# Second MoE layer in groups of four PSUM banks, with weight addresses kept in registers

## The chip, the cores and the metric

The kernel runs on one core of a Trainium2 chip. The metric is the device time of one execution in microseconds (us). Before the change it is 2098.32 us, the median of three runs (2098.08 to 2103.15). TensorE is called PE below (its weight loads PEld), VectorE DVE, ScalarE ACT, GpSimd POOL, SyncE SP.

## The reference

Three layers in a row over 14336 tokens of 192 numbers: a causal convolution with 7 softmax-normalised taps per head, a mixture of experts (MoE) in which each token goes to its best expert of eight, and a second MoE in which each token goes to its two best by noisy logits.

```python
x = _attn_ref(x, weight)                  # 7 taps, 8 heads of 24
# layer 1: expert_idx = argmax(x @ w_gate)
    h = np.maximum(xe @ w1[e], 0.0)       # 192 -> 1024
    out[mask] = gate_w * (h @ w2[e])      # 1024 -> 192
# layer 2: two best of logits + log1p(exp(x @ w_noise)) * noise
    h = np.maximum(x[mask] @ w1[e], 0.0)
    out[mask] += top2_w[mask, k, None] * (h @ w2[e])
```

All is float32, and the kernel gets near it with pairs of float16 numbers (a high and a low part).

## The kernel before

Tokens are scattered into DRAM tables with one region per expert (`rows1` for layer 1, `rows2` for layer 2), by POOL's indirect DMAs. A planner in the Python code (`spawn`, `pump`, `clk`) writes the order of every engine's instructions; a wait in that order is the hardware's. The MoE work runs as a list of steps (`seq`), each of T tokens of one expert: T is 512, 256 or 128. A step of layer 1 gets its rows as soon as an epoch of tokens is counted; layer 2 begins with four steps of 512 whose second weights have buffers of their own (`own`, the bridge), then 38 steps of 512 (19 regions of 1024), 7 of 512, 7 of 256 and 21 of 128. Layer 1 has 2 steps of 512, 45 of 256 and 21 of 128.

`load` (line 906) is SP's part of a step: the weights `w1t` (1 MB, three buffers), the tokens transposed into `xT` (three blocks of 128 rows: the high parts of inputs 0 to 127; high and low parts of inputs 128 to 191; low parts of 0 to 127), and, where `nb` is 2, `x3`, which holds the high parts of inputs 128 to 191 in its upper 64 rows.

`mm1` (line 939) makes the hidden layer. It has eight chunks of 128 hidden units. A chunk takes four matmuls over all 128 rows and one over the 64 rows that are left (low part of the weights by the high part of inputs 128 to 191). With `nb` 2 (all steps of layer 2 over 128 tokens, and the 512-token steps of layer 1) two chunks go to two PSUM banks `ph`, and their 64-row products stand next to each other, one on the lower 64 rows of the array and one on the upper, from `x3`. With `nb` 1 the fifth product is done over 128 rows. `parts` evicts a bank: ACT writes the relu as float16 into `h`, DVE the rest that float16 lost. There are four `ph` banks.

`mm2` (line 992) multiplies the step before by the second weights: per 128 tokens eight chunks of three matmuls, into a bank `py` (two of them). The weights of all experts lie in one tile `w2r`. Which expert it is is only known at run time: `st.re` is a register that PE loads from the table `g.tb` (`value_load`, line 947), and each matmul takes an address worked out from it. `run` (line 1160) alternates: a group of `mm1` for step n, a share of `mm2` for step n-1, then the evictions, then `finish`, where ACT scales `py` into `y` and POOL scatters it (layer 2: an adding scatter into the output; the first scatter of a step waits until those of the step before have landed).

Of the kernel before, what the change touches and what calls it, by code (L numbers as in the profile page):

```python
# [9 lines left out]
F16 = mybir.dt.float16  # L10
# [3 lines left out]
OP = mybir.AluOpType  # L14
# [4 lines left out]
P = 128  # L19
N, D, E, F = 14336, 192, 8, 1024  # L20
# [23 lines left out]
SLACK = {"dve": 0.4, "act": 0.4, "pool": 1.5, "pe": 1.2, "hw": 1.5, "dma": 6.0}  # L44
HOP = 0.15
BRIDGE = 4


def n_full(avail, t):
# [8 lines left out]
def conv_moe_moe2_kernel(ctx: ExitStack, tc: tile.TileContext, xh, cw, cwb, wg, w11, w21, w2t, w12, w22, out):  # L58
# [574 lines left out]
    def table(g, total):  # L633

        m, t, steps = g.m, g.t, g.k
        u = used[m][ucur[m]]
        L = lambda nm, shape=(P, E), dt=F32: sm.tile(list(shape), dt, name="tb" + nm, bufs=1)
        av = L("av")
        v.tensor_sub(av, total, u)
        yield vv()  # L640
        if g.last:
            v.tensor_scalar(av, av, float(t - 1), None, op0=OP.add)
            yield vv()
        ai = L("ai", dt=I32)
        v.tensor_copy(ai, av)
        yield vv()
        gi = L("gi", dt=I32)
        v.tensor_single_scalar(gi, ai, -t, op=OP.bitwise_and)
        yield vv()
        gf = L("gf")  # L650
        v.tensor_copy(gf, gi)
        yield vv()
        cm = L("cm", (P, E, E))
        v.tensor_tensor(cm, gf[:, None, :].to_broadcast([P, E, E]), upto, op=OP.mult)
        yield vv()
        ci = L("ci")
        v.tensor_reduce(ci, cm, op=OP.add, axis=AX.X)
        yield vv()
        cx = L("cx")
        v.tensor_sub(cx, ci, gf)  # L660
        pos = L("pos", (P, 1))
        v.tensor_scalar(pos, part, float(t), None, op0=OP.mult)
        yield vv()
        oh = L("oh")
        v.tensor_scalar(oh, ci, pos, None, op0=OP.is_gt)
        rb = L("rb")
        v.tensor_add(rb, u, reg_e)
        yield vv()
        v.scalar_tensor_tensor(oh, cx, pos, oh, op0=OP.is_le, op1=OP.mult)
        v.tensor_sub(rb, rb, cx)  # L670
        yield vv()
        val = L("val", (P, 4))
        v.scalar_tensor_tensor(cm[:, 0, :], rb, pos, oh, op0=OP.add, op1=OP.mult, accum_out=val[:, 0:1])
        v.scalar_tensor_tensor(cm[:, 1, :], iota_e, 1.0, oh, op0=OP.mult, op1=OP.mult, accum_out=val[:, 1:2])
        v.scalar_tensor_tensor(cm[:, 2, :], sE[m], 1.0, oh, op0=OP.mult, op1=OP.mult, accum_out=val[:, 2:3])
        yield vv()
        if g.last:
            v.tensor_reduce(val[:, 3:4], oh, op=OP.add, axis=AX.X)
            v.tensor_scalar(val[:, 3:4], val[:, 3:4], -float(DUMMY), float(DUMMY), op0=OP.mult, op1=OP.add)
            v.tensor_add(val[:, 0:1], val[:, 0:1], val[:, 3:4])  # L680
        tb = cst.tile([P, 3], I32, name=g.tag + "tb")
        v.tensor_copy(tb[:, 0:2], val[:, 0:2])
        v.tensor_scalar(tb[:, 2:3], val[:, 1:2], float(FC * 2 * DG), None, op0=OP.mult)
        dg = L("dg", (P, 2, steps))
        for j in range(2):
            v.tensor_scalar(dg[:, j, :], ident[:, :steps], val[:, 1 + j:2 + j], None, op0=OP.mult)
        yield vv()
        tk = L("tk")
        v.tensor_scalar(tk, cx, -1.0, float(steps * t), op0=OP.mult, op1=OP.add)
        v.scalar_tensor_tensor(tk, tk, 0.0, gf, op0=OP.max, op1=OP.min)  # L690
        nu = used[m][1 - ucur[m]]
        v.tensor_add(nu, u, tk)
        ucur[m] ^= 1
        g.tb, g.ready = tb, clk["dve"]
        yield on("pe", "dve")
        pb = yield from bank("pr")
        t_.matmul(pb[:, :2 * steps], ones32, dg.rearrange("p a b -> p (a b)"), start=True, stop=True)
        yield on("dve", "pe")
        g.bc = cst.tile([P, 2, steps], F32, name=g.tag + "bc")
        v.tensor_copy(g.bc.rearrange("p a b -> p (a b)"), pb[:, :2 * steps])  # L700
        held["pr"] = False
# [202 lines left out]
    def load(st):  # L904
        T, S = st.T, st.T // P
        g = st.g
        rows = rows1 if g.m == 0 else rows2
        rv = q_.value_load(g.tb[st.i:st.i + 1, 0:1], min_val=0, max_val=DUMMY if g.last else DUMMY - g.t)
        if st.first:
            re = q_.value_load(g.tb[st.i:st.i + 1, 1:2], min_val=0, max_val=E - 1)  # L910
            st.w[0] = wk.tile([P, 4 * F], F16, name="w1t", bufs=3)
            q_.dma_start(st.w[0], w1s[g.m].rearrange("e p f -> (e p) f")[bass.ds(re * P, P), :])
            if g.own:
                st.w[1] = prep[0].tile([P, FC * 2 * D], F16, name="w2t", bufs=BRIDGE)
                q_.dma_start(st.w[1], w2s.rearrange("e p f -> (e p) f")[bass.ds(re * P, P), :])
        row = bass.ds(rv + st.skip, T) if st.skip else bass.ds(rv, T)
        if st.off == 0:
            st.b.xT = wk.tile([P, 3, 512], F16, name="xT", bufs=3)
            st.b.ax = wk.tile([P, 4, AUX], F32, name="ax", bufs=9)
        st.xT = st.b.xT[:, :, st.off * P:st.off * P + T]  # L920
        ins = [q_.dma_start_transpose(st.xT, rows[row, 0:HALF].bitcast(F16))]
        if st.nb == 2:
            if st.off == 0:
                st.b.x3 = wk.tile([P, 512], F16, name="x3", bufs=3)
            st.x3 = st.b.x3[:, st.off * P:st.off * P + T]
            ins.append(q_.dma_start_transpose(st.x3[:, None, :], rows[row, 32:96].bitcast(F16)))
        st.ax = st.b.ax[:, st.off:st.off + S, :]
        ins.append(q_.dma_start(st.ax, rows[row, HALF:ROW].rearrange("(s p) w -> p s w", p=P)))
        for i in ins:
            row_read(g.m, i, g.deps)  # L930
        st.at = clk["done"]

    def chunk(st, k):

        n = 512 // st.T
        f, j = divmod(k, n)
        return f // st.nb * n + j + f % st.nb * FC // 2

    def mm1(st, f):


        T, n = st.T, 512 // st.T
        if f == 0:
            st.h = wk.tile([P, 2, 512 * FC // n], F16, name="h", tag="h", bufs=2)
            st.hv = st.h.rearrange("p k (c t) -> p k c t", c=FC)
        if f == st.nb % 2 and not st.g.own:
            st.re = t_.value_load(st.g.tb[st.i:st.i + 1, 2:3], min_val=0, max_val=(E - 1) * FC * 2 * DG)
        st.ph = [ps_h.tile([P, 512], F32, name="ph") for _ in range(st.nb)]
        x = lambda k: st.xT[:, k, :]
        for j in range(n):  # L950
            o = [ph[:, j * T:(j + 1) * T] for ph in st.ph]
            ws = []
            for b in range(st.nb):
                c = chunk(st, (f + b) * n + j)
                w = [st.w[0][:, k * F + c * P:k * F + (c + 1) * P] for k in range(4)]
                t_.matmul(o[b], w[0], x(0), start=True, stop=False)
                t_.matmul(o[b], w[0], x(2), start=False, stop=False)
                t_.matmul(o[b], w[1], x(0), start=False, stop=False)
                t_.matmul(o[b], w[2], x(1), start=False, stop=False)
                ws.append(w[3])  # L960
            if st.nb == 1:
                t_.matmul(o[0], ws[0], x(1), start=False, stop=True)
            else:
                t_.matmul(o[0], ws[0][:64], x(1)[:64], start=False, stop=True)
                t_.matmul(o[1], ws[1][64:], st.x3[64:], start=False, stop=True)

    def parts(st, f):
        hs = slice(f * 512, (f + 1) * 512)
# [7 lines left out]
    emptied = deque([0.0] * 4, maxlen=4)  # L976
    finished = []

    w2flat = w2r.rearrange("p e c -> p (e c)")

    def mm2(st, lo, hi):

        for qn in range(lo, hi):
# [3 lines left out]
            dd = D if st.g.m else DG  # L987
            py = st.py[:, :dd]
            hs = slice(s * P, (s + 1) * P)
            cw = chunk(st, c)  # L990
            if st.g.own:
                w = [st.w[1][:, (2 * cw + k) * D:(2 * cw + k + 1) * D] for k in range(2)]
            else:
                off = st.re + cw * 2 * dd
                w = [w2flat[:, bass.ds(off + k * dd if k else off, dd)] for k in range(2)]
            t_.matmul(py, st.hv[:, 0, c, hs], w[0], start=(c == 0), stop=False)
            t_.matmul(py, st.hv[:, 0, c, hs], w[1], start=False, stop=False)
            t_.matmul(py, st.hv[:, 1, c, hs], w[0], start=False, stop=(c == FC - 1))
# [156 lines left out]
    def run(seq):  # L1155
# [12 lines left out]
        for n, st in enumerate(seq + [None]):  # L1168
# [9 lines left out]
            for f in range(0, ns, nb):  # L1178
                ahead(n + 3)
                if st is not None:  # L1180
                    clk["pe"] = max(clk["pe"], emptied[nb - 1])
                    mm1(st, f)
                    if st.g.m and f == ns - nb:
                        ahead(n + 4)
# [23 lines left out]
    def group(m, t, k, last, own, tag):  # L1208
        g = Step()
        g.m, g.t, g.k, g.last, g.own, g.tag, g.tb, g.bc, g.deps = m, t, k, last, own, tag, None, None, None  # L1210
        for i in range(k):
            w = [None, None]
            for skip in range(0, t, 512):
                st = Step()
                st.g, st.T, st.i, st.skip, st.w, st.first, st.end = g, min(t, 512), i, skip, w, skip == 0, None
                st.nb = 2 if t > P and (m or t == 512) else 1
                S = st.T // P
                if not bats or bats[-1].S + S > 4:
                    bats.append(Batch())
# [139 lines left out]
```

## Time and profile before

| | |
|---|---|
| median of the runs | 2098.32 us |
| the profiled execution | 2103.14 us, span 2101.1 us |
| PE busy | 1796.6 us (86%), 16031 matmuls |
| DVE, ACT, POOL busy | 946.8, 848.5, 834.3 us |
| granted TensorE clock, mean | 0.91 |

The rows below are read so. A row of the timeline gives the start, the length, the engine, the operation with the tile it writes, an arrow and what it reads, and how many like it follow each other; in square brackets stands the idle time before it and what ended it. "issue" means that nothing the profile shows was waited for. A matmul's length contains the time in which it fills and drains the array, so a row of n matmuls is (n-1) steps and one length long. `ph<-xT,w1t` is mm1, `py<-w2r,h` is mm2, `ph<-x,w1t` is a product with `x3`.

### The profile page before, as it was taken

The page shows a single profiled execution, that of the slowest core. Times are in us where ns is not written, and L with a number is a line of the kernel's source. Part 1 is how long each engine was busy: PE and PEld are TensorE (multiplying, and loading weights), DVE is VectorE, ACT ScalarE, POOL GpSimd, SP SyncE. Part 2 cuts the span into 40 slices and gives each one's busy share as a digit, 9 for nine tenths or more (in the row PEclk, how much of TensorE's full clock was granted, in tenths as well). Part 3 has the DMA queues.
Part 4 walks back from the last instruction along what each step waited for, and adds up shares of the span by engine and source line. Part 5 has one row for each costly group of instructions (what it writes and reads, how often), then busy time and mean ns, then how long its engine had stood idle before and what let it go on. Part 6 is the DMA issues. An engine that isn't in the chain of part 4 may idle for free. (4 is left out here: it accounts for less than half of the span.)

```text
span 2101.1 us, 51695 instructions
## 1 busy us (share of the span) xinstructions
PE 1796.6 (86%) x16031; PEld 1365.3 (65%) x16031; DVE 946.8 (45%) x3508; ACT 848.5 (40%) x1756; POOL 834.3 (40%) x1512
## 2 busy tenths in 40 slices
PE   4778867667868897877789999999999999999993
PEld 3547756556757674766656666666666666667893
DVE  6856644535456574443345433333333333333341
ACT  4745644444334453433333333333333333333331
POOL 1453454545443334353335433333333333343323
PEclk9768988878879898888899999999999999999996
DMA  7868655334458785545698545554554556667792
GB/s 251 281 204 233 205 169 140 109 106 140 144 190 257 225 257 152 163 161 187 192 258 233 102 78 96 85 101 86 88 96 77 102 83 117 116 107 148 203 273 51
DMA packets 320693, 329.04 MB, mean 157 GB/s; under 512 B 230718, under 2 KB 279108, under 8 KB 303296
## 3 DMA queue, kind: packets, MB, share of 16 engines
q1 hardware_dynamic: 258400, 236.98, 40.2%
q0 software_dynamic: 55184, 74.92, 18.3%
q10 hardware_dynamic: 6864, 13.83, 2.0%
q8 instruction: 159, 2.61, 0.5%
q14 instruction: 86, 0.70, 0.1%
HBM read 189.50 MB, written 96.08 MB: 136 GB/s over the span
## 5 line engine op out<-in xcount | busy, mean ns | idle before, releaser
L95 PE MATMUL ph<-xT,w1t 128*128 128x256 f16 (+4 forms) x5568 | 877.0, 303 | 91.4 <-issue 78.7
L95 DVE SCALAR_TENSOR_TENSOR h<-ph,h 128x512 f16<-128x512 f32 x700 | 462.9, 687 | 961.1 <-ACT h L95 899.1
L95 PE MATMUL py<-w2r,h 128*128 x8016 | 813.5, 255 | 75.7 <-issue 74.4
L95 PEld LDWEIGHTS <-h 128*128 128x128 f16 x8400 | 726.2, 100 | 164.7 <-issue 146.8
L95 PEld LDWEIGHTS <-w1t 128*128 128x128 f16 (+1 forms) x5800 | 485.2, 101 | 398.0 <-issue 216.1
L95 ACT ACTIVATE h<-ph 128x512 f16<-128x512 f32 x700 | 392.3, 594 | 682.2 <-PE ph L95 493.7
L95 POOL DMA_INDIRECT out_dram<-y,ax x231 | 361.0, 1563 | 607.4 <-ACT y L95 421.3
L95 POOL DMA_INDIRECT rows<-row,gdi x238 | 237.3, 997 | 214.7 <-issue 189.0
L95 ACT ACTIVATE y<-py,cf 128x192 f32<-128x192 f32 (+1 forms) x350 | 148.6, 424 | 385.0 <-PE py L95 259.7
L95 POOL DMA_INDIRECT rows<-row,di x128 | 125.9, 984 | 152.2 <-DVE di L95 36.9
L95 POOL MEMSET spacer<- 1x1 f32 x613 | 172.4, 281 | 0.1
L95 PE MATMUL ph<-x,w1t 64*128 64x512 f16 (+1 forms) x232 | 87.3, 376 | 0.1
L95 PE MATMUL ph<-x,band 118*112 118x96 f32 x512 | 70.3, 299 | 5.2 <-issue 3.8
L95 PEld LDWEIGHTS ph<-x,band 118*112 118x112 f32 x512 | 66.4, 213 | 7.9 <-issue 5.5
L95 ACT ACTIVATE x<-x,ras 112x192 f32<-112x192 f32 x128 | 49.0, 446 | 19.3 <-DVE rai L95 13.2
L95 POOL CAST row<-gix 128x8 f32<-128x8 uint32 (+1 forms) x30 | 6.9, 229 | 110.0 <-DVE gex L95 47.0
L95 ACT ACTIVATE y<-y,rbs 128x192 f32<-128x192 f32 x119 | 46.5, 445 | 6.9 <-DVE rbs L95 6.9
L95 ACT ACTIVATE rT<-ph 128x672 f16<-128x672 f16 x64 | 43.2, 729 | 15.0 <-PE ph L95 10.7
L95 PE MATMUL ph<-ident,row 112*128 112x112 f16 x384 | 33.3, 245 | 15.4 <-DVE row L95 6.4
L95 PEld LDWEIGHTS <-row 112*128 112x128 f16 x384 | 27.6, 116 | 21.5 <-issue 12.7
L95 DVE TENSOR_TENSOR row<-x,row 112x256 f16<-112x256 f32 x64 | 33.4, 554 | 13.1 <-ACT row L95 12.9
L95 ACT ACTIVATE x<-ph 112x384 f32<-112x384 f32 x64 | 28.2, 480 | 27.0 <-PE ph L95 13.5
(275 smaller groups left out, 1142.6 us busy)
## 6 DMA issues: line engine op xcount, KB each, us to landing
w1t<-w1s SPq DMA_DIRECT2D x126, 1024.0 KB
x<-in_xh_dram ACTq DMA_DIRECT2D x32, 400.0 KB
w1raw<-in_w_dram SPq DMA_DIRECT2D x8, 1536.0 KB
w2raw<-in_w_dram SPq DMA_DIRECT2D x16, 768.0 KB
out_dram<-pads SPq DMA_DIRECT2D x11, 960.0 KB
w1s<-w1raw POOLq DMA_DIRECT2D x16, 512.0 KB
w1s<-whalf SPq DMA_DIRECT2D x16, 512.0 KB
w2tr<-in_w2t_dram POOLq DMA_DIRECT2D x16, 384.0 KB
```

The source lines that it names most:

```text
L95: r = f(*a, **kw)
```

## The change

Steps of layer 2 over 128 tokens take four chunks to four banks at a time (`nb` 4). The four 64-row products of both pairs of chunks stand in the middle of the group: chunks 0 and 1, then lower, upper, lower, upper rows, then chunks 2 and 3. The two 512-token steps of layer 1 get `nb` 1: no 64-row products and no `x3`. The order of chunks is now plain, so `chunk` is gone. The table's third column holds a byte offset. After the first two matmuls of a step, PE loads it and works out 16 addresses into 16 registers (`addresses`); an mm2 matmul then takes its address from a register as it stands. The planner's `emptied[nb // 3]` looks at the second of the last four evictions for `nb` 4.

```diff
+W2_AT = 20480
...
-        v.tensor_scalar(tb[:, 2:3], val[:, 1:2], float(FC * 2 * DG), None, op0=OP.mult)
+        v.tensor_scalar(tb[:, 2:3], val[:, 1:2], float(4 * FC * DG), None, op0=OP.mult)
...
-        if st.nb == 2:
+        if st.nb == 4:
...
-    def chunk(st, k):
-
-        n = 512 // st.T
-        f, j = divmod(k, n)
-        return f // st.nb * n + j + f % st.nb * FC // 2
-
     def mm1(st, f):
...
-        if f == st.nb % 2 and not st.g.own:
-            st.re = t_.value_load(st.g.tb[st.i:st.i + 1, 2:3], min_val=0, max_val=(E - 1) * FC * 2 * DG)
         st.ph = [ps_h.tile([P, 512], F32, name="ph") for _ in range(st.nb)]
         x = lambda k: st.xT[:, k, :]
+
+        def w(b, j, k):
+            c = (f + b) * n + j
+            return st.w[0][:, k * F + c * P:k * F + (c + 1) * P]
+
+        out_ = lambda b, j: st.ph[b][:, j * T:(j + 1) * T]
+        def whole(b):
+            for j in range(n):
+                o = out_(b, j)
+                first = j == 0 and b < 2
+                t_.matmul(o, w(b, j, 0), x(0), start=first, stop=False, skip_group_check=True)
+                t_.matmul(o, w(b, j, 0), x(2), start=False, stop=False, skip_group_check=True)
+                if f == b == j == 0 and not st.g.own:
+                    addresses(st)
+                t_.matmul(o, w(b, j, 1), x(0), start=False, stop=False, skip_group_check=True)
+                t_.matmul(o, w(b, j, 2), x(1), start=False, stop=b > 1, skip_group_check=True)
+
+        if st.nb == 4:
+            whole(0)
+            whole(1)
+            for b in (0, 2):
+                for j in range(n):
+                    for i, (rows, src) in enumerate(((slice(0, 64), x(1)), (slice(64, P), st.x3))):
+                        t_.matmul(out_(b + i, j), w(b + i, j, 3)[rows], src[rows], start=b == 2 and j == 0,
+                                  stop=b == 0, skip_group_check=True)
+            whole(2)
+            whole(3)
+            return
         for j in range(n):
-            o = [ph[:, j * T:(j + 1) * T] for ph in st.ph]
-            ws = []
-            for b in range(st.nb):
-                c = chunk(st, (f + b) * n + j)
-                w = [st.w[0][:, k * F + c * P:k * F + (c + 1) * P] for k in range(4)]
-                t_.matmul(o[b], w[0], x(0), start=True, stop=False)
-                t_.matmul(o[b], w[0], x(2), start=False, stop=False)
-                t_.matmul(o[b], w[1], x(0), start=False, stop=False)
-                t_.matmul(o[b], w[2], x(1), start=False, stop=False)
-                ws.append(w[3])
-            if st.nb == 1:
-                t_.matmul(o[0], ws[0], x(1), start=False, stop=True)
-            else:
-                t_.matmul(o[0], ws[0][:64], x(1)[:64], start=False, stop=True)
-                t_.matmul(o[1], ws[1][64:], st.x3[64:], start=False, stop=True)
+            o = out_(0, j)
+            t_.matmul(o, w(0, j, 0), x(0), start=True, stop=False)
+            t_.matmul(o, w(0, j, 0), x(2), start=False, stop=False)
+            if f == j == 0 and not st.g.own:
+                addresses(st)
+            t_.matmul(o, w(0, j, 1), x(0), start=False, stop=False)
+            t_.matmul(o, w(0, j, 2), x(1), start=False, stop=False)
+            t_.matmul(o, w(0, j, 3), x(1), start=False, stop=True)
 
...
-    w2flat = w2r.rearrange("p e c -> p (e c)")
+    w2bytes = w2r.rearrange("p e c -> p (e c)").bitcast(mybir.dt.uint8)
+
+    def addresses(st):
+
+        pe = nc.tensor
+        first = pe.value_load(st.g.tb[st.i:st.i + 1, 2:3], min_val=0, max_val=4 * (E - 1) * FC * DG)
+        step = 2 * (D if st.g.m else DG)
+        st.wr = []
+        for k in range(2 * FC):
+            r = pe.alloc_register(f"w2at{len(addressed)}_{k}")
+            pe.reg_alu(r, first, W2_AT + k * step, op=OP.add)
+            st.wr.append(pe.snap(r, min_val=W2_AT, max_val=W2_AT + 4 * (E - 1) * FC * DG + k * step,
+                                 guaranteed_mod_val=0, out_of_modulus=32))
+        addressed.append(st)
+
+    addressed = []
 
     def mm2(st, lo, hi):
 
...
-            cw = chunk(st, c)
+            cw = c
             if st.g.own:
                 w = [st.w[1][:, (2 * cw + k) * D:(2 * cw + k + 1) * D] for k in range(2)]
             else:
-                off = st.re + cw * 2 * dd
-                w = [w2flat[:, bass.ds(off + k * dd if k else off, dd)] for k in range(2)]
+                w = [w2bytes[:, bass.ds(st.wr[2 * cw + k] - W2_AT, 2 * dd)].bitcast(F16) for k in range(2)]
             t_.matmul(py, st.hv[:, 0, c, hs], w[0], start=(c == 0), stop=False)
             t_.matmul(py, st.hv[:, 0, c, hs], w[1], start=False, stop=False)
             t_.matmul(py, st.hv[:, 1, c, hs], w[0], start=False, stop=(c == FC - 1))
...
-                    clk["pe"] = max(clk["pe"], emptied[nb - 1])
+                    clk["pe"] = max(clk["pe"], emptied[nb // 3])
...
-                st.nb = 2 if t > P and (m or t == 512) else 1
+                st.nb = 4 if m and t > P else 1
```

The instructions on PE at the start of a 512-token step of layer 2, where mm2 of the step before ends and mm1 begins; `ISA` is a register instruction. Before:

```order
L95 LDWEIGHTS h
L95 ISA
L95 MATMUL py<-w2r,h 128x192
L947 TENSOR_LOAD tb1024tb
L947 ISA x2
L95 LDWEIGHTS w1t
L95 MATMUL ph<-xT,w1t 128x512
L95 LDWEIGHTS w1t
L95 MATMUL ph<-xT,w1t 128x512
L95 LDWEIGHTS w1t
```

The same place now:

```order
L96 LDWEIGHTS w1t
L96 MATMUL ph<-xT,w1t 128x512
L96 LDWEIGHTS w1t
L96 MATMUL ph<-xT,w1t 128x512
L998 TENSOR_LOAD tb1024tb
L998 ISA x2
L96 LDWEIGHTS w1t
L1003 ISA
L1004 ISA
L1003 ISA
L1004 ISA
L1003 ISA
```

The register instruction ahead of each mm2 matmul is gone, and the load of the expert's offset, with seven register instructions instead of two, has moved behind two matmuls of mm1.

The 64-row products of a 512-token step on PE, from the last 128-row product ahead of them; the rows with `x` read `x3`. Before, where mm2 follows:

```order
L95 LDWEIGHTS w1t
L95 MATMUL ph<-xT,w1t 128x512
L95 LDWEIGHTS w1t
L95 MATMUL ph<-xT,w1t 128x512
L95 LDWEIGHTS w1t
L95 MATMUL ph<-x_20971,w1t 128x512
L95 LDWEIGHTS h
L95 ISA
L95 MATMUL py<-w2r,h 128x192
L95 LDWEIGHTS h
```

Now, where four such products stand together and mm1 goes on:

```order
L96 MATMUL ph<-xT,w1t 128x512
L96 LDWEIGHTS w1t
L96 MATMUL ph<-xT,w1t 128x512
L96 LDWEIGHTS w1t
L96 MATMUL ph<-x_24917,w1t 128x512
L96 LDWEIGHTS w1t
L96 MATMUL ph<-xT,w1t 128x512
L96 LDWEIGHTS w1t
L96 MATMUL ph<-x_24917,w1t 128x512
L96 LDWEIGHTS w1t
L96 MATMUL ph<-xT,w1t 128x512
L96 LDWEIGHTS w1t
```

A switch from 128-row to 64-row products and back stood after every two chunks, and stands after every second pair of them now.

## Rows read from the trace of the kernel before

**Rows 1.** The page of the profile: its head and the engines' busy time.

```profile
span 2101.1 us, 51695 instructions
...
PE 1796.6 (86%) x16031; PEld 1365.3 (65%) x16031; DVE 946.8 (45%) x3508; ACT 848.5 (40%) x1756; POOL 834.3 (40%) x1512
```

**Rows 2.** Busy time by stretches: start:end, length, five engines, PE clock, DMA share, GB/s.

```profile
1400.00:1500.00 100.00, 100.00 (x820) 66.55 (x820) 34.09 (x66) 36.34 (x73) 38.69 (x50) 1.00 0.52 89
```

**Rows 3.** The timeline of large steps of layer 2, a group of mm1 and mm2.

```profile
1404.03 2.15 PE L95 MATMUL py<-w2r,h 128*128 x24
1404.13 1.08 ACT L95 ACTIVATE h<-ph 128x512 f16<-128x512 f32 x2 [1.62 <-PE ph L95]
1404.76 1.29 DVE L95 SCALAR_TENSOR_TENSOR h<-ph,h 128x512 f16<-128x512 f32 x2 [2.85 <-ACT h L95]
1405.94 1.48 PEld L95 LDWEIGHTS <-w1t 128*128 128x128 f16 x8
...
1406.02 1.89 PE L95 MATMUL ph<-xT,w1t 128*128 128x512 f16 x8
...
1407.84 0.10 PEld L95 LDWEIGHTS <-w1t 64*128 64x128 f16 x2 [0.42 <-issue]
...
1411.98 0.39 PE L95 MATMUL ph<-xT,w1t 64*128 64x512 f16 x1
1411.98 0.39 PE L95 MATMUL ph<-x,w1t 64*128 64x512 f16 x1
1412.30 2.15 PE L95 MATMUL py<-w2r,h 128*128 x24
1414.36 2.21 PE L95 MATMUL ph<-xT,w1t 128*128 128x512 f16 x9
```

**Rows 4.** Groups of PE instructions by shape, whole span: count, busy us, mean ns, idle before.

```profile
L95 PE MATMUL ph<-xT,w1t 128*128 128x512 f16 x1632 | 391.0, 382 | 5.1 <-issue 4.7
L95 PE MATMUL ph<-xT,w1t 128*128 128x128 f16 x1680 | 121.5, 227 | 32.9 <-issue 30.4 <-PE py L95 0.5 <-PE pr L95 0.3
...
L95 PE MATMUL ph<-xT,w1t 64*128 64x256 f16 x28 | 7.8, 280 | 0.0
```

**Rows 5.** The timeline of PE in the 256-token steps of layer 2.

```profile
1906.49 4.90 PE L95 MATMUL py<-w2r,h 128*128 x48
1911.94 0.81 PE L95 MATMUL ph<-xT,w1t 128*128 128x256 f16 x6 [0.56 <-DMA w1t<-w1s]
```

**Rows 6.** The timeline of PE and POOL in the 128-token steps that end layer 2.

```profile
2024.11 1.15 PE L95 MATMUL py<-w2r,h 128*128 x12
2025.37 1.29 PE L95 MATMUL ph<-xT,w1t 128*128 128x128 f16 x20
...
1979.29 1.56 POOL L95 DMA_INDIRECT out_dram<-y,ax  x1 [2.80 <-ACT y L95]
...
2061.85 1.56 POOL L95 DMA_INDIRECT out_dram<-y,ax  x1 [2.63 <-ACT h L95]
...
2092.53 1.56 POOL L95 DMA_INDIRECT out_dram<-y,ax  x1 [3.32 <-issue]
```

**Rows 7.** Waits of PE from 250 to 1150 us: total us, times, longest.

```profile
PE ph L95 <- issue: 83.4, 115, 1.9
PE py L95 <- issue: 73.2, 95, 1.8
```

**Rows 8.** The timeline of PE and POOL over one of those stretches.

```profile
1008.20 1.23 PE L95 MATMUL py<-w2r,h 128*128 x12
1009.60 0.28 PE L95 MATMUL ph<-xT,w1t 128*128 128x128 f16 x2 [0.16 <-issue]
...
1013.39 0.22 PE L95 MATMUL ph<-xT,w1t 128*128 128x128 f16 x1 [1.21 <-issue]
...
1017.70 1.03 PE L95 MATMUL ph<-xT,w1t 128*128 128x128 f16 x8 [0.44 <-issue]
...
1006.05 0.99 POOL L95 DMA_INDIRECT rows<-row,gdi  x1 [6.13 <-issue]
...
1015.24 0.99 POOL L95 DMA_INDIRECT rows<-row,gdi  x1 [0.23 <-issue]
```

## The prediction

> **What bounds the kernel now.** I read the stretches first, then the timeline of the stretch with the most time, then the waits of PE, then the end. In layer 2 the stretch of 100 us has PE busy for all of it at clock 1.00, the others for 34 to 39 us [rows 2]. So from about 1150 to 1970 us time is what PE's instructions take one after another. In layer 1 PE is also what the order waits for, but with holes: from 250 to 1150 us it idles 83.4 + 73.2 = 156.6 us for nothing that the profile shows [rows 7]. One such hole runs from 1009.60 to 1017.70: a matmul or two in each 0.7 us or so [rows 8]. Over it POOL issues eight scatters back to back, 1006.05 to 1016.23 [rows 8]. The very end is neither: POOL's adding scatters of the 128-token steps wait for one another, 13 intervals from 1979.29 to 2061.85 at 6.35 us and 7 more to 2092.53 at 4.38 us [rows 6]. I work against the profiled execution, 2103.14 us (span 2101.1 [rows 1] and 2.0 outside); it is 4.8 us over the median of 2098.32, and a saving is taken off that median.
>
> **64-row products, large steps.** A full 512-column matmul takes (1.89 - 0.38)/7 = 0.216 us; 0.38 is one matmul's mean length [rows 3, 4]. The eighth should make way at 1406.02 + 8 x 0.216 = 1407.75, but the weights of the 64-row products are only loaded at 1407.84 [rows 3]: 0.095 us. The two products start together at 1411.98, and mm2 follows at 1412.30: 0.32 us for 0.216 us of columns, 0.104 us more [rows 3]. So a pair costs 0.216 us and its two edges 0.20. Now two pairs share the edges: 0.20 us less in each group of four, 0.40 in a step. There are 1632/32 = 51 steps of 512 [rows 4], 49 of them in layer 2: **19.6 us**. The two of layer 1 pay 40 full matmuls (8.64 us) where they paid 32 and four pairs with edges (8.58): nothing.
>
> What the trace of before does not show is one 64-row pair right behind another. If the second costs as much as the first with its edges, the gain is 0; if its weights are loaded behind the running pair, it is the 19.6. At full height the loads do run ahead: eight of them lie between 1405.94 and 1407.42, beside the matmuls of the same rows [rows 3]. That row is the nearest, so I take 19.6. [...]
>
> **Smaller steps of layer 2.** A 256-token step has four pairs (28 products of a kind in 7 steps [rows 4]), each with its edges before, and one run of four now: 3 x 0.20 x 7 = **4.2 us**.
>
> **Register instructions.** Each mm2 matmul had one ahead of it. In large steps that is hidden: 24 matmuls pass in 1.99 us, 0.083 each, their 192 columns' worth at the rate above [rows 3]. In a run of 48 it is not: (4.90 - 0.25)/47 = 0.099 [rows 5]. The new group has runs of 48 everywhere; without the instruction I put them at 0.083, with no gain or loss.
>
> Loading the offset stood between mm2 and mm1. There mm1 starts 2.06 us after mm2 did, against 1.99 [rows 3]: 0.07 us in each of 45 large steps, **3 us**. In 128-token steps the hole is larger: 2024.11 + 12 x 0.083 = 2025.11, and mm1 starts at 2025.37 [rows 6], 0.27 us. If layer 1's 21 such steps pay alike, as 1008.20 to 1009.60 for twelve matmuls says [rows 8], that is **5.7 us** on PE there. The 7 steps of 256 give about 1.9 at that price, less what a wait for `w1t` as at 1911.94 takes back [rows 5]: I keep **1**. The 21 steps at the end gain 5.7 on PE too, but POOL's chain behind them sets the end: **1**.
>
> The load now stands behind two matmuls, with five more register instructions. I cost it at nothing, because behind an mm2 without register instructions PE's queue should hold enough work. If that cover fails, it costs the 0.27 us hole plus five instructions at no more than 0.099 us, 0.77 us in each of 141 steps: 109 us. Ends 0 and 109; the large step, with 0.07 us left uncovered under the old load [rows 3], is the nearest row, and there the queue was fed more slowly than it will be.
>
> **Evictions.** Four banks instead of two now wait for ACT and DVE. Two take ACT 1.08 us and DVE 1.29 [rows 3], four about 3.2 with the first relu. The first two banks are complete in the middle of the group; the last one is done about 1.5 us after the group's end, and PE then has 48 mm2 matmuls, 4.0 us, before it needs banks 0 and 1. No wait; without that cover it would be up to 1.5 us in each of 98 groups. The `y` copies come behind the evictions on ACT, and their scatters behind them; POOL is busy 39 of 100 us [rows 2].
>
> **Holes of layer 1.** In a hole the instructions come at a fixed poor rate, so their number counts. mm2 falls from three per matmul to two: a third of its 73.2 us would be 24 us [rows 7], while mm1's 83.4 stays. A hole's end follows POOL's last scatter (1016.23, then 1017.70 [rows 8]), which the change does not touch, so I take half, **12 us**. Bounds: 0, and all 156.6.
>
> Sum: 19.6 + 4.2 + 3 + 5.7 + 1 + 1 + 12 = 46.5 us. 2098.3 - 46.5 = **2052 us** (the profiled execution would be 2057).
>
> **Rivals.**
> 1. The second pair pays its own edges: 19.6 + 4.2 = 24 us less gain, **2076**. For it: both edges stand at every pair in the trace. Against it: the edge comes with the change from 128 rows to 64, and between pairs there is none.
> 2. The queue carries PE through the holes. Without register instructions it is full when a hole begins, and PE works from it. About ten waits make a hole [rows 8], so 210 waits are some 21 holes [rows 7]. If what it holds more than before is worth one mm2 block of 24 matmuls, 1.99 us [rows 3], 21 holes give 42 us more: **2010**. For it: holes begin at once where mm2 with its register instructions has just passed (1008.20, then 1009.60). Against: no row shows what is queued. [...]
> 3. Slower: the address block is uncovered, 109 us as above, with 19.6 + 4.2 + 12 = 36 us gained beside it: 73 us more, **2171**. It decides from 36/141 = 0.26 us of hole per step. For it: the hole of 0.27 us already there in 128-token steps [rows 6]. Against: that hole comes where register instructions slow the queue's filling.
> 4. PE's gains do not reach the end: layer 1 waits for its scatters, and the chain on POOL [rows 6] starts no earlier, **2095**. Against it: PE had no other wait of size in layer 1, and the chain's first scatter waits for a `y` that PE makes.
>
> **Chances.** Forecast 0.60, rival 1 0.17, rival 2 0.12, rival 3 0.06, rival 4 0.05. About 0.3% (6 us) is what a measurement of this kernel tells from no change. Faster by more: the first three cases, 0.88 with something off for smaller mishaps; within 0.3%: 0.05; slower: 0.07. Range: 2016 to 2081, which takes in rival 1 and most of the way to rival 2, with 2040 to 2065 for the forecast's own case.
>
> **What would show it.** Large steps: a step's period, 4 x (1.99 + 8 x 0.216 + 0.42) + 0.07 = 16.6 us by [rows 3], should be 16.2, with the third 64-row product 0.216 us behind the first and a full matmul 0.32 us behind the third. If the third starts 0.4 us behind the first, rival 1 holds. At a step's start, mm1's third matmul should follow the second after one column time; a hole there is rival 3. In layer 1, PE's issue waits should fall from 157 us to some 140; to 100 or less is rival 2. The scatters at the end should be the same chain, begun about 46 us earlier. I am wrong at the root if PE is not busy throughout layer 2 any more, for then a bank, an `h` or a `w1t` is waited for.

## The result, and the profile after

The changed kernel takes **2053.81 us** (median of 2052.87, 2053.42, 2054.19 and 2055.71) against 2098.61 us of the kernel before beside it: ratio 0.978, interval 0.977 to 0.980, 44.8 us saved. Its profiled execution is 2054.19 us, 48.95 under the one of before, which was 4.5 us over its median.

The page's head, for [rows 1]: the span, and PE's busy time, which falls by 39 us for the same 16031 matmuls.

```profile
span 2052.3 us, 44340 instructions
PE 1757.6 (86%) x16031; PEld 1369.5 (67%) x16031; DVE 947.4 (46%) x3508; ACT 861.0 (42%) x1756; POOL 839.6 (41%) x1512
```

The same stretch as in [rows 2]: PE is still busy throughout at clock 1.00, and gets 833 matmuls done where it did 820.

```profile
1400.00:1500.00 100.00, 100.00 (x833) 67.81 (x832) 34.94 (x68) 38.86 (x75) 40.03 (x50) 1.00 0.57 95
```

A group of a large step, for [rows 3], from PE's timeline, with the loads of the four 64-row weights at its end. The products of the second pair start at 1401.36, 0.22 us behind the first; a full matmul follows 0.31 us later. All four loads lie between 1401.13 and 1401.24, the second pair's beside the running first pair. A matmul's length in this trace and that of before is 0.163 us over its step, in the median, at 128 columns (0.219 and 0.056), 256 (0.273 and 0.109) and 512 (0.379 and 0.216); that this is the array filling and draining is not shown.

```profile
1399.30 2.23 PE L96 MATMUL ph<-xT,w1t 128*128 128x512 f16 x9
1401.14 0.39 PE L96 MATMUL ph<-x,w1t 64*128 64x512 f16 x1
1401.36 0.38 PE L96 MATMUL ph<-xT,w1t 64*128 64x512 f16 x1
1401.37 0.38 PE L96 MATMUL ph<-x,w1t 64*128 64x512 f16 x1
1401.67 1.90 PE L96 MATMUL ph<-xT,w1t 128*128 128x512 f16 x8
...
1401.13 0.11 PEld L96 LDWEIGHTS <-w1t 64*128 64x128 f16 x4 [0.42 <-issue]
```

The first 256-token step, for [rows 5]: its two runs of 48 mm2 matmuls, 4.9 us each, are one of 96 in 8.08, 0.082 a matmul.

```profile
1855.93 8.08 PE L96 MATMUL py<-w2r,h 128*128 x96
```

The 128-token steps, for [rows 6]: the hole ahead of mm1 is gone, and a larger one stands behind its second matmul: the third starts 0.57 us behind the first, where two matmuls take 0.11. Below it the chain of scatters at the end: 12 intervals from 1927.21 to 2008.73 at 6.79 us, 8 more at 4.41.

```profile
1971.10 1.15 PE L96 MATMUL py<-w2r,h 128*128 x12
1972.09 0.28 PE L96 MATMUL ph<-xT,w1t 128*128 128x128 f16 x2
1972.66 1.17 PE L96 MATMUL ph<-xT,w1t 128*128 128x128 f16 x18 [0.30 <-issue]
...
1927.21 1.56 POOL L96 DMA_INDIRECT out_dram<-y,ax  x1 [4.11 <-DMA out_dram<-y,ax]
...
2008.73 1.56 POOL L96 DMA_INDIRECT out_dram<-y,ax  x1 [7.01 <-issue]
...
2043.99 1.56 POOL L96 DMA_INDIRECT out_dram<-y,ax  x1 [2.61 <-issue]
```

PE's waits from 250 to 1150 us, for [rows 7]: 143.7 us where they were 156.6.

```profile
PE ph L96 <- issue: 77.7, 114, 1.8
PE py L96 <- issue: 66.0, 89, 1.8
```

Each step has 40 matmuls of mm1, so the trace gives the start of each of the 145 steps. By stages, in us from the first mm1 matmul of one stage to that of the next (for the last stage, to the start of PE's last matmul). The last four columns are explained with the experiments; "holes" are stretches like that of [rows 8], and the last column is from a chip that has them:

| stage (steps) | before | changed | before, no holes | changed, no holes | spread, no holes | spread + pause |
|---|---|---|---|---|---|---|
| layer 1, 256 and 512 (47) | 770.0 | 743.9 | 574.6 | 571.5 | 570.1 | 613.6 |
| layer 1, 128 (21) | 157.6 | 155.0 | 104.8 | 105.9 | 100.0 | 115.5 |
| layer 2, bridge and two more (6) | 101.3 | 106.4 | 96.1 | 94.2 | 92.4 | 96.9 |
| layer 2, 512 (43) | 715.2 | 694.3 | 715.1 | 694.0 | 692.9 | 692.9 |
| layer 2, 256 (7) | 69.3 | 62.4 | 69.3 | 62.4 | 60.7 | 60.7 |
| layer 2, 128 (21) | 100.2 | 102.4 | 100.3 | 102.5 | 95.8 | 97.5 |
| ahead of and behind them | 187.5 | 187.8 | 186.6 | 195.5 | 197.2 | 198.5 |

So 28.7 of the 48.8 us of span come from layer 1, 20.9 from the large steps (0.486 each), 6.9 from the 256-token steps; the bridge gives 5.1 back and the last 128-token steps 2.2.

### The profile page after: what moved, and what is told of

Read it like the earlier page. It is cut to its first block, busy times and chain, and to the rows that moved or that the text cites. A ratio compares the mean times of both kernels' runs of the same rounds, so it can differ in the third digit from the quotient of the medians.

```text
span 2052.3 us, 44340 instructions
## 1 busy us (share of the span) xinstructions
PE 1757.6 (86%) x16031; PEld 1369.5 (67%) x16031; DVE 947.4 (46%) x3508; ACT 861.0 (42%) x1756; POOL 839.6 (41%) x1512
## 5 line engine op out<-in xcount | busy, mean ns | idle before, releaser
L96 PE MATMUL ph<-xT,w1t 128*128 128x256 f16 (+3 forms) x5576 | 868.1, 302 | 94.5 <-issue 84.4
L96 PE MATMUL py<-w2r,h 128*128 x8016 | 789.9, 254 | 66.0 <-issue 65.8
L96 PEld LDWEIGHTS <-h 128*128 128x128 f16 x8400 | 738.6, 100 | 132.8 <-issue 90.1
L96 PEld LDWEIGHTS <-w1t 128*128 128x128 f16 (+1 forms) x5800 | 477.3, 101 | 387.6 <-issue 212.5
L96 ACT ACTIVATE h<-ph 128x512 f16<-128x512 f32 x700 | 404.1, 594 | 539.6 <-PE ph L96 360.5
L96 PE MATMUL ph<-x,w1t 64*128 64x512 f16 (+1 forms) x224 | 63.7, 370 | 2.6 <-issue 2.6
L96 ACT ACTIVATE x<-x,ras 112x192 f32<-112x192 f32 x128 | 49.0, 447 | 16.9 <-DVE rai L96 10.8
L96 PE MATMUL pl<-oneoa,rT 128*112 128x16 f16 (+1 forms) x256 | 28.6, 202 | 11.0 <-remote 4.7
```

Source lines behind the costliest of these rows:

```text
L96: r = f(*a, **kw)
```

## The experiments

The runs were made on four chips, each kernel beside the kernel before. On two of the chips that one took 1845 and 1850 us, on the other two 2080 and 2100, as in the runs above. "No holes" means the former; times are compared within a set of runs, by the ratio to the kernel before on the same chip. Stages and steps come from one profiled execution of each kernel.

**Before and after once more**, as they are.

> The kernel before, for its trace beside the runs of this study, in which its time was 1845 us and not 2098. Theory: what is gone are the holes of layer 1 (PE's waits for nothing shown between 250 and 1150 us, 156.6 us in the trace of before, and the low clock behind them), everything else stands: a large step 16.62 us, a 128-token step of layer 2 4.47 us, layer 1's 68 steps over by about 840 us instead of 1080. Rival: the large steps differ as well.

> The changed kernel as it is, beside the kernel before at 1845 us. Theory: of the 44.8 us, what layer 1 gave (29.6 us up to the first step of layer 2) came from its holes, and where there are none only layer 2 gains: 0.48 us in each of 45 large steps, 6.9 us in the 256-token steps, less about 0.2 us in each of the 42 steps of 128: 1845 - 18 = about 1827 us, ratio about 0.990. Rival: layer 1 gains as much without holes, through its two 512-token steps and the fewer instructions: 1800 us, ratio 0.976.

The profiled execution of before took 1848.7 us; the changed kernel takes 1829.37, ratio 0.989 (0.986 to 0.993) to the 1849.77 of before. The waits of PE from 250 to 1150 us, before and then changed:

```profile
PE ph L95 <- issue: 1.1, 4, 0.4
```

```profile
PE ph L96 <- issue: 15.4, 33, 1.7
```

The holes are not there, though POOL's scatters come as closely as ever: the median interval within the bursts is 1.29 us here and 1.28 in the trace of [rows 8]. Here, in the timeline of before, PE works on in 128-token steps while eight scatters pass, the last 9.23 us behind the first (in [rows 8] it was 9.19):

```profile
744.84 1.23 PE L95 MATMUL py<-w2r,h 128*128 x12
745.90 1.28 PE L95 MATMUL ph<-xT,w1t 128*128 128x128 f16 x20
747.02 1.23 PE L95 MATMUL py<-w2r,h 128*128 x12
...
744.87 1.00 POOL L95 DMA_INDIRECT rows<-row,gdi  x1 [2.27 <-issue]
...
754.10 0.98 POOL L95 DMA_INDIRECT rows<-row,gdi  x1 [0.22 <-issue]
```

The 15.4 us that the changed kernel waits here are its own: most of them come from the block of register instructions behind mm1's second matmul, and with that block taken apart (below) 2.2 are left.

Layer 1 takes 679.4 us instead of 927.7, and the change gains 2.0 us in it instead of 28.7. Layer 2's stages are the same to 0.3 us, the bridge apart. So most of layer 1's gain exists only where there are holes, and without it the change is worth some 20 us.

**The pairs apart**, each with its own edges:

```diff
-            for b in (0, 2):
-                for j in range(n):
...
-            whole(2)
-            whole(3)
+            pair(0)
+            whole(2)
+            whole(3)
+            pair(2)
```

> The changed kernel with its two pairs of 64-row products apart, one in the middle of the group and one at its end, so that each pair has its own way in and out of 64 rows. Theory: the edges are 0.20 us a pair, so each group costs 0.20 us more, 2 groups in 49 large steps and one in each of 7 steps of 256 (there two pairs on either side): 19.6 + 1.4 us, about 2075 us, a large step 16.53 instead of 16.13 us. Rival: a pair's edges are hidden when mm1 stands on both sides of it or the saving of the large steps came from the long mm2 runs: 2054 to 2060.

1847.62 us, ratio 1.001 (0.998 to 1.004), where the change has 0.989: 1.15%, 21 us. That the 21 us expected came is in part chance: in the profiled execution the large steps take 18.4 us more than the changed kernel's and the 256-token steps 1.6, but layer 1 takes 14.5 more and what lies ahead of and behind the stages 11 less, which the edit does not explain. The reading rests on the steps: large ones take 16.57 us, 0.43 more than the changed kernel's 16.14. In its timeline both pairs have their edges: 0.32 us from a pair to what follows, and mm2 in 3.97 us as in the changed kernel.

```profile
1311.09 0.39 PE L96 MATMUL ph<-x,w1t 64*128 64x512 f16 x1
1311.41 2.22 PE L96 MATMUL ph<-xT,w1t 128*128 128x512 f16 x9
1313.24 0.39 PE L96 MATMUL ph<-x,w1t 64*128 64x512 f16 x1
1313.56 4.13 PE L96 MATMUL py<-w2r,h 128*128 x48
1317.53 2.23 PE L96 MATMUL ph<-xT,w1t 128*128 128x512 f16 x9
```

So 0.43 of the 0.486 us that a large step gains are the edges.

**Registers alone**, in pairs of banks:

```diff
-        if f == st.nb % 2 and not st.g.own:
-            st.re = t_.value_load(...)
...
+                if f == b == j == 0 and not st.g.own:
+                    addresses(st)
...
-                off = st.re + cw * 2 * dd
-                w = [w2flat[:, bass.ds(off + k * dd if k else off, dd)] for k in range(2)]
+                w = [w2bytes[:, bass.ds(st.wr[2 * cw + k] - W2_AT, 2 * dd)].bitcast(F16) for k in range(2)]
```

> Registers alone: the kernel before, in pairs of banks as it was, with the 16 addresses worked out behind the first two matmuls of a step. Theory: the saving of layer 1 belongs to the registers, the saving of the large steps mostly to the groups. Then layer 1 is left some 25 to 29 us earlier than before, large steps go from 16.62 to about 16.55 us each (the 0.07 us hole, 3 us in all), the 128-token steps of layer 2 take 4.69 instead of 4.47 us, and the time is about 2070 us. Rival A: layer 1 gains only its part of the waits for nothing shown, 13 us (156.6 to 143.7): about 2084. Rival B: layer 1's saving comes from its two 512-token steps and the order that the groups give: about 2095.

1857.44 us, 0.7% slower: 1.007 (1.005 to 1.009), on a chip without holes. A large step takes 16.74 us, 0.11 more than before, since the block makes mm1's third matmul late by 0.07 to 0.42 us, 0.21 in the median of 43 steps, in place of the old hole ahead of the first, 0.08 in the median; a 128-token step takes 4.67 to 4.72, as expected. What the expectations say of layer 1 could not show on this chip; what the theory says of the large steps, 16.55 us, failed.

**Groups alone**, with an address per matmul as before (the reverse of the lines above, in the changed kernel).

> Groups of four alone: the changed kernel with the offset loaded and an address worked out ahead of each mm2 matmul as before. Theory: the groups need the registers. A run of 48 mm2 matmuls with a register instruction each goes at 0.099 us a matmul instead of 0.083, 0.77 us more in each of 2 groups in 45 large steps, 69 us more, against 19.6 + 4.2 us of edges saved: about 2144 us, slower than before; a large step takes about 17.8 us. Rival: the edges' gain does not depend on how the addresses come, and the queue carries the long run: 2098 - 24 = about 2074, a large step about 16.2.

1862.59 us, 1.0% slower: 1.010 (1.006 to 1.013). The sign was as expected, the size (2144) was not: large steps take 16.89 us, not 17.8. The run of 48 is not slowed as in [rows 5]: it takes 4.12 us here. But its register instructions come 0.124 us apart in the trace and its matmuls 0.083, so in 48 they fall back behind the matmuls by 48 x 0.041, some 2.0 us, and the load of the offset behind the run (taken up at 1303.99, its last register instruction done at 1304.62) is bare. The view puts the wait down to a DMA, yet it stands in every large step:

```profile
1303.80 0.49 PE L96 MATMUL py<-w2r,h 128*128 x4
1304.68 2.22 PE L96 MATMUL ph<-xT,w1t 128*128 128x512 f16 x9 [0.39 <-DMA x<-rows]
```

mm1 starts at 1304.68, where four matmuls at 0.083 end at 1304.13: 0.55 us, at the next step's 0.73, 0.64 in the median of 43. Each part alone is slower than the kernel before; together they gain.

**The block taken apart**, in groups of four: the load where it is, four addresses behind each of four chunks.

```diff
+    def more(st, c):
+
+        if st.g.own or c % 2:
+            return
...
+        for k in range(len(st.wr), len(st.wr) + 4):
```

> The changed kernel with its address block taken apart: the load behind the first two matmuls as it is, and four addresses behind each of the 1st, 3rd, 5th and 7th chunk of mm1. Theory: the block as one piece is longer than what PE's queue holds in a 128-token step and makes a hole of 0.46 to 0.58 us there. Taken apart, the hole goes: 128-token steps of layer 2 fall from 4.69 to about 4.2 us and the undisturbed ones of layer 1 from 4.91 to about 4.4. The ones of layer 2 stand before the chain of scatters and give nothing, the 21 of layer 1 up to 8 us: about 2047 us. Rival: layer 1's 128-token steps are paced by the bursts of scatters and its 256-token steps are not touched: 2053, no change.

> The kernel with the spread addresses once more, beside the changed kernel on one chip. Theory: 21 steps of 128 in layer 1 at 0.45 us less each, the 256-token steps 0.1 to 0.25 us less each, 10 to 15 us under the changed kernel: 1810 us, ratio to before about 0.981. The 9 us that PE gains in layer 2's 128-token steps are lost again before the chain of scatters. Rival: what layer 1 gains is taken up by waits for rows and only 3 us remain.

1810.12 and 1810.59 us, ratios 0.980 (0.976 to 0.984) and 0.980 (0.977 to 0.983), beside 0.989 of the changed kernel: 18.8 us less than it on the same chip, and the version that beats both. PE's timeline in the 128-token steps has no hole left:

```profile
1677.39 1.28 PE L96 MATMUL ph<-xT,w1t 128*128 128x128 f16 x20
1678.50 1.15 PE L96 MATMUL py<-w2r,h 128*128 x12
1679.49 1.28 PE L96 MATMUL ph<-xT,w1t 128*128 128x128 f16 x20
```

Such a step is 4.21 us, expected 4.2, until `w1t` loads slow some. The gain of the last 128-token steps is not lost before the chain of scatters, against both expectations: PE ends 16.3 us earlier, the span 16.9.

**Registers alone, taken apart.** The same edit in pairs of banks.

> Registers alone with the addresses spread: the kernel before, in pairs of banks, the load behind the first two matmuls of a step and four addresses behind each of four later chunks. Theory: registers alone gained nothing because their block took the place of the old load's hole; without a block large steps go to 16.55 us (4 x 4.13 us, no hole; 16.63 before, 16.74 with the block), the 128-token steps to 4.21 us (4.47 before), the 256-token ones of layer 2 to 8.5: some 3 + 4 + 6 us in layer 2 and 3 in layer 1, 1845 - 14 = about 1831 us. Rival: the per-matmul register instruction was hidden in pairs of banks and nothing is gained, 1845. What the groups then add is the difference to the spread version in groups of four, 1810.

On a chip with holes: 2053.69 us, before 2080.2, ratio 0.986 (0.981 to 0.991). Large steps take 16.54 us and 128-token steps 4.21 until loads slow them, as expected. Layer 2's four stages sum to 973.4 us, 12.6 less than in before's trace (from another chip with holes); the other 14 of the 26.5 us saved lie outside them. In layer 1 PE waits for nothing shown for 48.6 us ahead of mm2 and 77.5 ahead of mm1, where before's trace has 74.4 and 81.9.

**A pause between scatters.** If the holes come from bursts of scatters, spacing these must end them.

```diff
+    pause = cst.tile([1, 512], F32, name="pause")
...
         g_.memset(spacer, 0.0)
+        if not kw.get("compute_op"):
+            g_.memset(pause, 0.0)
```

> The changed kernel with a memset of 512 numbers on POOL ahead of each scatter of rows, some 0.7 us, so that a burst of eight scatters takes about 16 us instead of 10. Where PE's instructions stall during such bursts, theory: they no longer do, and PE's waits for nothing shown between 250 and 1150 us fall from 144 us to under 60; rival: the stall comes with each scatter and stays. Where there are no holes, both expect the same: 382 scatters at 0.7 us more on POOL, which is busy about half of layer 1, so 0 to 30 us slower than the changed kernel.

1999.26 us, far off 1829 and what either expected, on a chip without holes. The new tile moved `w2r` by 2048 bytes, its address was no longer `W2_AT`, and PE got an arithmetic instruction ahead of each of 8016 mm2 matmuls again: large steps of 17.14 us. So it was tried again with the tile behind `w2r`.

> The changed kernel with the memset of 512 numbers ahead of each scatter of rows, its tile placed behind w2r, so that w2r keeps its address and the mm2 matmuls take their registers as they stand. Theory: of the 170 us that the first try with a pause cost, some 1.0 us a large step (43 us in 43 steps) and much of the 128- and 256-token steps came from the ALU instruction per mm2 matmul that the moved address brought; with the pause alone large steps are 16.13 us again. Layer 1 keeps its part (about 67 us to the first step of layer 2, and 60 in the bridge): about 1940 us. Rival: the pause itself slows layer 2, and its large steps stay at 17.1. If PE stalls in bursts of scatters here, the pause removes these stalls.

On a chip with holes: 1924.72 us, before 2080.2; large steps 16.15 us, as expected, and PE's waits for nothing shown are down to 25 us. But two waits, of 45 us for `xT` and of about 50 in the bridge, came with the planner's new order. In the last two runs the pause is hidden from the planner (`nc.gpsimd.memset`), in the kernel with spread addresses.

> Spread addresses in groups of four, and a memset of 512 numbers on POOL ahead of each scatter of rows that the planner does not count, so that the order of every engine stays that of the spread version. Theory: the holes come with scatters 1.29 us apart and not with 1.70 us, and the 46 and 52 us that the pause cost were the planner's new order. Where the kernel before takes some 2080 to 2098 us, this one takes about 1830, ratio 0.88; where it takes 1847, there are no holes to remove, and the longer bursts (4 us each) cost some 0 to 10 us against 1810. Rival: the waits of 46 and 52 us come from POOL's own time, and it takes 1910 us on either.

> The same with a memset of 128 numbers, some 0.2 us, scatters about 1.4 us apart. Theory: if the stall comes from scatters issued faster than they are worked off, a part of the holes stays, PE's waits for nothing shown in layer 1 between the 141 us of the changed kernel and none: 1850 to 1980 us where the kernel before takes 2080 to 2098. Rival: any instruction more between two scatters ends them, 1830 us as with the long pause. Where there are no holes: 1810, as the spread version.

Before took 2099.8. With 512 numbers, scatters 1.69 us apart: **1874.23 us**, ratio 0.892 (0.887 to 0.896). With 128, 1.37 us apart: 2037.57, ratio 0.967 (0.962 to 0.972). Two scatters in POOL's timeline, and PE's waits from 250 to 1150 us, with 512:

```profile
604.09 0.99 POOL L96 DMA_INDIRECT rows<-row,gdi  x1 [0.17 <-issue]
605.78 0.97 POOL L96 DMA_INDIRECT rows<-row,gdi  x1 [0.17 <-issue]
```

```profile
PE ph L96 <- issue: 4.6, 10, 1.1
PE py L96 <- issue: 2.0, 2, 1.5
```

and with 128:

```profile
603.05 0.98 POOL L96 DMA_INDIRECT rows<-row,gdi  x1 [0.17 <-issue]
604.41 0.98 POOL L96 DMA_INDIRECT rows<-row,gdi  x1 [0.17 <-issue]
```

```profile
PE py L96 <- issue: 67.8, 115, 1.2
PE ph L96 <- issue: 59.0, 108, 1.2
```

At 1.37 us the holes are there, at 1.69 they are not, with the same instructions on PE: the bursts make them. The long pause gives 1874, between the 1830 of the theory and the 1910 of the rival. The bridge is back from 157.1 to 96.9 us, so its part was the planner's order. Layer 1 takes 729.1 us, 59 more than the spread version's on a chip without holes. These 59 are not holes: PE idles 37 us more, but waits for nothing shown for 5.0 us where that version has 2.5, and it is busy for 22 us more at a mean granted clock of 0.92 instead of 0.96. POOL is busy for 536 us instead of 391, and the first try has 734 us in layer 1 on a chip without holes, though with its extra instructions. That the pause's own time on POOL makes the 59 us is likely by this, and not shown: the spread version with the pause was not run on a chip without holes.

## Why the prediction was right, and where its terms were not

2052 us was forecast and 2053.81 came, but partly because errors cancelled: layer 1 was to give 17.7 us and gave 28.7, while the bridge and the last 128-token steps took 7.3 back.

1. **Edges, 19.6 us, and the hole of the large steps, 3 us: right.** 0.47 us a step was forecast, 0.486 measured, and the pairs apart put 0.43 back. Rival 1 falls with the third product's 0.22 us: its weights were loaded, by 1401.24, beside the first product on the same rows, which started 0.22 us ahead of the third and takes 0.39.
2. **256-token steps, 4.2 + 1: right where they were counted, one run left out.** 6.9 came. With spread addresses such a step takes 8.74 us in pairs and 8.10 in groups: 0.64 for three sets of edges, 4.5 us in seven steps. Registers without a block are worth another 0.31 (9.05 to 8.74), of which the block takes back 0.24 (8.34 to 8.10). That makes 0.7 a step. The first one gained 2.7, because its runs of 48 [rows 5] no longer have a register instruction to each matmul: 1.6 us that the forecast named and left out of its sum.
3. **128-token steps of layer 1, 5.7, and the address block at nothing: wrong.** This is the failed step: "PE's queue should hold enough work". The block takes some 1.7 us in the trace, with 0.22 us from one of its register instructions to the next, where the forecast's own worst case allowed 0.099. When PE takes up the block's load, 17 matmuls ahead of mm1's third have not begun, in each of 45 large steps and in 18 of the 21 128-token steps that end layer 2. In a large step these are 15 of mm2 and two of mm1, at 0.083 and 0.216 us some 1.68 us, and they cover nearly all of it: the third is late by 0.02 to 0.12 us, 0.03 in the median, behind mm2 runs of 48, and by 0.21 in the median behind runs of 24 (registers alone). In a 128-token step they are 12 of mm2 and five of mm1, at 0.083 and 0.056 some 1.28 us, and the hole is 0.46 us in the rows above (0.34 to 0.59 in the 21 steps that end layer 2) for the old 0.27. In the median such steps went from 4.66 to 4.88 us in layer 1 (without holes) and from 4.49 to 4.71 in layer 2. Rival 3 was to decide from 0.26 us of hole a step, 36 us in all, and without holes from scatters the block makes about that: 18.8 us in layer 1's 47 steps of 256 and 512, 9.2 in its 21 of 128, 1.4 in the large steps, 1.7 in the seven of 256 and 10.3 in the last 21, against 1.0 in all in the trace of before. So its hole was there, but not its price, as a part of it falls where other waits would have stood. Taking the block apart removes some 35 us of these holes and gave 18.8, of which the stage of layer 1's 47 steps has only 1.5.
4. **Holes, 12 us: the fall of the waits right in amount, partly by luck; what it gives mis-sized.** PE's waits fell by 12.9 us, to 143.7 where some 140 were forecast. But the forecast took all of it from the waits ahead of mm2, and these fell by 7.2 us only; those ahead of mm1, which were to stay, fell by 5.7. And layer 1 as a whole gave 28.7: 14.8 of such waits ahead of mm1 and mm2 within its own bounds, 9.0 of PE's busy time (721.8 to 712.8 us, the mean granted clock 0.85 and 0.87) and 4.9 of other waits, most of them for nothing shown too. On a chip without holes 2.0 of it is left. The forecast counted the waits and not the low clock beside them: on the chip without holes the same stretch of before has 0.95. The bridge's loss of 5.1 us looks like a hole too: PE stalls from 1119 to 1125 us behind a burst of scatters of pads, the last at 1120.60, where the old order had lost 1.2; without holes the bridge gains 1.9.
5. **The end, 1: right.** Same chain, its scatters begun 52 us earlier and ended 48.5 earlier. On the chip without holes 8 us of PE's 29 were lost there: two scatters more were left for the time behind the loads (ten intervals of 4.2 to 4.9 us instead of eight).
6. **Rival 2** (the queue carries PE through the holes, 42 us more) is not borne out: waits did not fall to 100. **Rival 4** falls with the result.

What stays open: why two chips of the four show the holes and two do not, and how a burst of scatters keeps PE's instructions back. That fewer instructions on PE shorten the holes fits layer 1's gain of 28.7 us with holes and 2.0 without. Registers alone, taken apart, comes nearest to varying their number by itself: there the waits ahead of mm2 are a third shorter and those ahead of mm1 nearly as before, just as the forecast reasoned. But the trace of before is from another chip, and the spread version with the short pause, with as few instructions per mm2 matmul but longer bursts, has 67.8 us ahead of mm2 again. So how the holes' length hangs on the number of instructions is not shown.

## What to carry to other kernels

Price a block of register instructions against the time of the matmuls that have not begun when it is taken up (here 17: 1.68 us in a large step, 1.28 in a 128-token one), in the shortest step and not in the commonest, and spread it where that time is short. Two edits to one engine's instructions must be tried together and apart: here each alone, as written, was slower by 0.7 and 1.0%, and both together gained 1.1% on such a chip. A gain that sits in stalls of one trace may not exist on another chip, so split the forecast into what a busy engine saves and what a stall gives back.

## What the runs showed of the hardware

Scatters issued by POOL every 1.28 to 1.37 us hold back PE's instructions, to one or a few in 0.7 us [rows 8], on some chips: from 250 to 1150 us PE waits for nothing shown for 156.6 us in the kernel before, 143.7 in the changed one and 126.8 with the short pause, and the kernel before has a granted clock of 0.85 in layer 1, where it has 0.95 on a chip without holes. At 1.69 us apart they do not (6.6 us), on a chip that has the holes at 1.37; and on a chip without holes scatters 1.29 us apart left 1.1 us. The same program took 1849 us on one chip and 2103 on another; 248 us of the difference lie in layer 1 (679 against 928), while layer 2's large steps agreed to 0.01 us each. And a new tile of 2 KB moved another tile off the address that a constant assumes, which put an instruction ahead of 8016 matmuls and showed only as time (large steps of 17.14 us instead of 16.14).
